# One core, attention and two gated layers: the small inverses' products issued alternately, and an order of issue of its own for every attention row

## The chip, the cores and the metric

One core of a Trainium2 chip. The time is the device time of one execution in microseconds (us). Engines: TensorE (PE, its weight loads PEld), VectorE (DVE), ScalarE (ACT), GpSimd (POOL), SyncE (SP, which issues most DMAs). Each engine works through its own queue in order.

## What is computed

A delta-rule attention over 4 x 8 heads, 768 steps, head size 48, then two feed-forward layers over 3072 tokens of width 384.

```python
for t in range(S):                                   # attention, k normalised
    y[:, :, t] = q[:, :, t] @ state
    v_old = k_n[:, :, t] @ state
    state += beta[:, :, t] * outer(k_n[:, :, t], v[:, :, t] - v_old)
...
xn = x / rms * rms_g                                 # layer 1: 384 -> 1536 -> 384
x = (silu(xn @ w_gate) * (xn @ w_val)) @ w_out
...
h = x @ w_in                                         # layer 2: 384 -> 2048 -> 384
out = (h * tanh(softplus(h))) @ w_out
```

The weights arrive as 64-bit floats and are split on the chip into a high and a low 32-bit part; each large product is three matmuls (high x high, low x high, high x low).

## The kernel before

The 768 steps are cut into 12 rows of 64 steps (r = 0 to 11), two rows making a group (sg = 0 to 5). Inside a row the recurrence becomes the inverse of a 64x64 triangular matrix per head, 32 of them, built from the Gram matrix of the keys (`products`, L578). The inverse of the 32x32 diagonal blocks is built lane by lane on VectorE, and 32x32 products on TensorE put the blocks together:

- For groups 0 and 1 `quick_lane` (L761) goes only to 16x16 blocks on VectorE; `quick_products(r)` (L847) then makes the rest on TensorE in five steps: off x Yd and `Zq` (L861 to L865, with one VectorE addition); YT x Zq (two strips, L867), two copies on ScalarE; Zq x YT (strips 32 and 96, L879) with two copies, and the opening product of `merge32` (L739) with two copies; Zq x YT (strips 0 and 64, L884) with two copies; the closing product of `merge32` (L749) with two copies, which sets ("Y", r).
- For groups 2 to 5 `inlane` (L631) makes 32x32 blocks on VectorE, and `merges` (L890) runs `merge32` for both rows of the group: open, close, open, close, each 32 products and two copies. These steps are called from within `lanes` (L897), one for every two units of the next group's lane.

A product of 32 rows occupies one of four 32-row strips of the array (partitions 0, 32, 64, 96). `merge32` uses two strips at a time, off x Yd all four.

`chain_row(r)` (L914) is a row of attention in named stages: q0, q1 (transposes of q), r (residual), y (state x q), p (masked scores: L600 on TensorE, mask L610 on VectorE), v (`values`, needs ("Y", r)), o0, o1 (outputs), k (state update), s and x (scaling and transposes to the layer's input, done a row later as S, T, X, Y), nA, nB (norms of row r+4's keys), c0, c1, g (its transposes and Gram products). The order of the stages is the string of P: R0, R1, R2, ROW for rows 3 to 9, RL for 10 and 11.

The order of issue is written out by a planner. For rows 0 and 1 `plan` (L44) always issues the stream with the lowest due time; the due times stand in P (`ROW0`, `ROW1`, `QP` for `quick_products`, `L` for the two quick lanes, `CV` for weight conversion, `FF` for part A). From row 2 on `merge` (L62) interleaves streams in proportion to their totals: the row, part A's budget (`DUE`), the conversion of weights, and the lane (`until`, with total `LANE`). Part A is the first third of layer 1 (two of the six slices of 256 hidden columns, gate, value and output weights) for all 12 blocks of 256 tokens; it runs between the attention's products. Weight conversion (`prepare_half`, L152) takes a half at a time: load, absolute value (ScalarE, L168), four operations on VectorE (L172 to L183), the high part cast (ScalarE, L194) and the low part (GpSimd or VectorE, L197). In rows 10 and 11 and the tail it converts the rest of layer 1's weights, which phase B (`phase_b2`, the other four slices) uses from about 460 us on; phase C (layer 2) follows.

Of the kernel before, what the change touches and what calls it, by code (L numbers as in the profile page):

```python
# [20 lines left out]
    XB=2, WE=16, RB=4, TB=4, LANE=18.8, AFTER=6.2, LD=3.0, CVT=9.0, CVB0=0, CVB1=64.0, PSD=1, NU=4, LAG=4, XD=9, PD=12, SQ=5,  # L21
    ROW="r nA q0 q1 S p T nB y X v Y k c0 o0 c1 o1 g".split(),
    R0="r q0 q1 p v k o0 o1 s0 s1 x0 x1 c0 c1 g".split(),
    R1="r nA q0 q1 y p nB v k o0 o1 s0 s1 x0 c0 c1 g".split(),
    R2="r nA Y q0 q1 p nB y v k c0 o0 c1 o1 g".split(),
    RL="r q0 q1 S p T y X Y v o0 k o1".split(),
    DUE=[0, 6, 5, 11],
    CVS=[0, 0, 6.5, 0],
    C=dict(n=0.2, q=0.5, r=1.4, y=1.1, p=1.2, v=1.2, o=0.9, k=1.2, s=0.1, x=0.45, c=0.4, d=0.4, g=1.2, h=1.2),

    ROW0=[24.0, 24.1, 24.4, 46.4, 46.6, 48.6, 49.5, 50.0, 51.0, 51.5, 52.0, 54.0, 62.0, 62.5, 90.0],
    ROW1=[52.5, 54.5, 55.0, 55.5, 56.0, 57.0, 60.0, 60.5, 62.5, 63.5, 64.0, 65.0, 65.5, 66.0, 84.0, 84.5, 90.5],
# [5 lines left out]
    CV=[21.0, 22.0, 23.0, 73.2, 74.8, 76.4, 77.8, 77.9, 78.0] + [79.5 + 0.9 * i for i in range(40)],  # L38
    K1=[7.3, 9.95, 10.0, 10.6], K23=[11.95, 13.2, 15.1, 16.0], K4=[30.0, 47.0, 50.2, 53.0], S=[0, 11.0, 22.0, 23.0, 54.0],
    T=[9.9, 13.0, 25.5, 26.0], G=[12.0, 15.0, 27.5, 28.0], BL=29.0, CVN=12.9,  # L40
# [58 lines left out]
def kernel(  # L99
# [243 lines left out]
    def phase_b1():  # L343
# [234 lines left out]
        def products(r):  # L578
            if r >= NR:
                return  # L580
            sg, rl = divmod(r, 2)
            if rl == 0:
                need(*([("v", r - 5)] if sg > 2 else []))
                A_t[sg] = As[sg % 3]
            need(("T", r, 0), ("T", r, 1))
            gram(("G", r), kT_t[r], kT_t[r], None, A_t[sg][:, rl * 16:rl * 16 + 16, :], swap=True)
            yield 1
# [143 lines left out]
        def merge32(r, X11, Z):  # L731
# [4 lines left out]
            for i in range(16):  # L736
                for e in range(2):
                    o = e * 64
                    nc.tensor.matmul(  # L739
                        ps[o + 32:o + 64, i, :], A[o:o + 32, rl * 16 + i, 32:64], X11[o:o + 32, i, :]  # L740
                    )
            for o in (32, 96):
                nc.scalar.copy(Z[o:o + 32], ps[o:o + 32])
            yield 1.5
            ps = bank(16, 32)
            for i in range(16):
                for e in range(2):
                    o = e * 64
                    nc.tensor.matmul(  # L749
                        ps[o:o + 32, i, :], Z[o + 32:o + 64, i, :], A[o + 32:o + 64, rl * 16 + i, 32:64]  # L750
                    )
# [3 lines left out]
            yield 1.5  # L755

# [4 lines left out]
        def quick_lane(sg):  # L761
# [14 lines left out]
            offs = [t[:, 544:1056].rearrange("p (u c) -> p u c", c=32) for t in (N_, X_)]  # L776
            for rl in range(2):
# [31 lines left out]
            for rl in range(2):  # L809
                r = 2 * sg + rl  # L810
                Nv, Xv = Nw[:, rl], Xw[:, rl]
                for x, y, d in (
# [30 lines left out]
                )  # L843
                halves[r] = [t.rearrange("p (u c) -> p u c", c=32) for t in (Yd, YT)] + [offs[rl]]
                yield 1.75

        def quick_products(r):  # L847
# [5 lines left out]
            def small(lhsT, rhs, groups=(0, 32, 64, 96), ps=None):  # L853
                if ps is None:
                    ps = bank(16, 32)
# [535 lines left out]
```

## Time and profile before

| | us |
|---|---|
| median of 3 runs (lowest, highest) | 1177.6 (1176.66, 1181.1) |
| profiled execution | 1181.6 |
| its span, first to last instruction | 1179.9 |
| TensorE busy in the span | 1112.7 (94%) |
| VectorE, ScalarE, GpSimd busy | 615.0, 387.3, 408.4 |
| mean granted TensorE clock | 0.949 |

A granted clock of 1.00 is 2.4 GHz, of 0.50 is 1.2 GHz; a value between is a mixture over the stretch. Matmuls are pipelined, so an engine that shows busy all the time may still be waiting for the rate of issue. In a line such as `L858 PE MATMUL pp<-A,Zq`, L858 is the line of the kernel, pp the tile written, A and Zq the tiles read; a 32-bit product shows as two records, so a pass of 32 products in the code counts 64. "issue" is a wait for nothing that the profile shows. An interval in brackets at the end of a row is idle time before it and what ended it.

### The profile page before, as it was taken

Reading aid. Unit: us, or ns where it says so; the run is one execution under the profiler, and the core shown is the slowest. Engines: PE = TensorE matmul, PEld = TensorE weight load, DVE = VectorE, ACT = ScalarE, POOL = GpSimd, SP = SyncE. Lnnn points to the kernel's source line nnn. Section 1 sums busy time; section 2 is a strip of 40 time slices with the busy share of each in tenths; the row PEclk is TensorE's granted clock in tenths of the full one; section 3 lists DMA queues with packets and bytes.
Section 4 is the critical chain, followed back from the end, with each engine's and each line's share of the span. In section 5 each row is a group of like instructions: output and inputs, shape, how many; then the busy total and the mean of one; then the engine's idle time right before and its main releaser. Section 6 shows DMA issues by size and latency. Waiting matters only on the chain.

```text
span 1179.9 us, 33143 instructions
## 1 busy us (share of the span) xinstructions
PE 1112.7 (94%) x14712; PEld 1083.1 (92%) x14712; DVE 615.0 (52%) x1039; ACT 387.3 (33%) x822; POOL 408.4 (35%) x364
## 2 busy tenths in 40 slices
PE   5678779999999889999999999999999999999998
PEld 5677678989898889999999999999999999999998
DVE  6656798898987988777676732221111111111111
ACT  4365735676656663222222210111111111111110
POOL 2021035455432442444444432243333333333331
PEclk8656788999999999999999999999999999999999
DMA  9031323333324554443446432611110101111101
GB/s 165 3 70 42 111 56 83 83 90 80 80 83 132 155 203 159 127 142 122 130 139 204 159 122 81 228 54 41 41 41 31 27 25 41 41 41 41 41 1 27
DMA packets 130847, 104.48 MB, mean 89 GB/s; under 512 B 81008, under 2 KB 113264, under 8 KB 130704
## 3 DMA queue, kind: packets, MB, share of 16 engines
q1 hardware_dynamic: 118608, 78.77, 24.0%
q10 hardware_dynamic: 12096, 23.60, 6.1%
q8 instruction: 115, 1.88, 0.7%
q14 instruction: 28, 0.23, 0.1%
HBM read 69.31 MB, written 33.03 MB: 87 GB/s over the span
## 4 chain that ended last, share of the span: by engine, by line
PE 79%; DVE 14%; ACT 2%; SPq 2%; issue 2%; POOL 1%; DMA 0%; DVEq 0%; POOLq 0%; ACTq 0%
PE ph L260 6%; PE ph L259 6%; PE ph L261 6%; PE pd L1322 6%; PE pd L1323 6%; PE pd L1321 6%; PE pg L259 4%; PE pv L259 4%; PE pd L293 4%; PE pg L260 4%; PE pg L261 4%; PE pd L294 4%; PE pd L295 4%; PE pv L261 4%; PE pv L260 4%; DVE pr L658 2%
## 5 line engine op out<-in xcount | busy, mean ns | idle before, releaser
L1309 POOL TENSOR_TENSOR gl<-t,gh 128x512 fp32r<-128x512 f32 x96 | 123.9, 1291 | 266.0 <-DVE gh L1308 266.0
L1308 DVE CAST gh<-t 128x512 fp32r<-128x512 f32 x96 | 43.5, 456 | 328.8 <-ACT t L1303 328.8
L321 POOL TENSOR_TENSOR hl<-sg,hh 128x512 fp32r<-128x512 f32 x72 | 104.5, 1451 | 231.2 <-DVE hh L320 229.8
L1303 ACT ACTIVATE t<-ph 128x512 f32<-128x512 f32 x96 | 57.5, 599 | 346.7 <-PE ph L261 343.1
L260 PE MATMUL ph<-xl,wih 128*128 128x256 f32 x576 | 161.7, 281 | 0.0
L259 PE MATMUL ph<-xh,wih 128*128 128x256 f32 x576 | 161.6, 281 | 0.0
L261 PE MATMUL ph<-xh,wil 128*128 128x256 f32 x576 | 161.5, 280 | 0.0
L1322 PE MATMUL pd<-wql,gh 128*128 128x384 f32 x384 | 129.7, 338 | 0.0
L1323 PE MATMUL pd<-wqh,gl 128*128 128x384 f32 x384 | 129.6, 338 | 0.0
L1321 PE MATMUL pd<-wqh,gh 128*128 128x384 f32 x384 | 129.5, 337 | 0.0
L259 PE MATMUL pv<-xh,wvh 128*128 128x256 f32 x432 | 127.0, 294 | 2.2 <-DVE sg L317 2.2
L259 PE MATMUL pg<-xh,wgh 128*128 128x256 f32 x432 | 127.1, 294 | 0.0
L260 PE MATMUL pg<-xl,wgh 128*128 128x256 f32 x432 | 123.4, 286 | 1.4 <-POOL xl L1071 1.3
L261 PE MATMUL pg<-xh,wgl 128*128 128x256 f32 x432 | 123.0, 285 | 1.5 <-DVE wgl L197 1.5
L261 PE MATMUL pv<-xh,wvl 128*128 128x256 f32 x432 | 123.2, 285 | 1.2 <-DVE wvl L197 1.2
L293 PE MATMUL pd<-hh,woh 128*128 128x256 f32 x420 | 120.5, 287 | 3.0 <-DVE xl L1063 1.5
L260 PE MATMUL pv<-xl,wvh 128*128 128x256 f32 x432 | 123.0, 285 | 0.0
L311 ACT ACTIVATE sg<-pg 128x512 f32<-128x512 f32 x72 | 43.2, 601 | 236.5 <-PE pg L261 215.9
L294 PE MATMUL pd<-hl,woh 128*128 128x256 f32 x420 | 119.0, 283 | 0.0
L295 PE MATMUL pd<-hh,wol 128*128 128x256 f32 x420 | 118.7, 283 | 0.0
L261 PEld LDWEIGHTS ph<-xh,wil 128*128 128x128 f32 x576 | 108.6, 188 | 0.0
L260 PEld LDWEIGHTS ph<-xl,wih 128*128 128x128 f32 x576 | 108.4, 188 | 0.0
(208 smaller groups left out, 2617.7 us busy)
## 6 DMA issues: line engine op xcount, KB each, us to landing
raw<-in_moe_w_out_dram SPq DMA_DIRECT2D x28, 384.0 KB, 3.1
raw<-in_moe_w_in_dram SPq DMA_DIRECT2D x16, 384.0 KB, 4.5
kh<-in_k_dram SPq DMA_DIRECT2D x24, 192.0 KB, 3.9
qp<-in_q_dram SPq DMA_DIRECT2D x24, 192.0 KB, 3.6
v<-in_v_dram SPq DMA_DIRECT2D x48, 96.0 KB, 3.1
raw<-in_moe_w_gate_dram SPq DMA_DIRECT2D x12, 384.0 KB, 4.0
raw<-in_moe_w_val_dram SPq DMA_DIRECT2D x12, 384.0 KB, 3.6
xh_d<-xh SPq DMA_DIRECT2D x12, 384.0 KB, 2.4
```

The source lines that it names most:

```text
L259: nc.tensor.matmul(ps[:, f, :], wh[:, kt, sl], xh[:, kt, :], start=(kt == 0), stop=False)
L260: nc.tensor.matmul(ps[:, f, :], wh[:, kt, sl], xl[:, kt, :], start=False, stop=False)
L261: nc.tensor.matmul(ps[:, f, :], wl[:, kt, sl], xh[:, kt, :], start=False, stop=(kt == KD - 1))
L293: nc.tensor.matmul(ps, wh[:, f, sl], hh[:, f, :], start=(i + f == 0), stop=False)
L294: nc.tensor.matmul(ps, wh[:, f, sl], hl[:, f, :], start=False, stop=False)
L295: nc.tensor.matmul(ps, wl[:, f, sl], hh[:, f, :], start=False, stop=last)
L321: nc.gpsimd.tensor_tensor(out=hl, in0=sg, in1=hh.bitcast(F32), op=ALU.subtract)
L1303: nc.scalar.activation(out=t, in_=ps, func=ACTF.Mish)
L1309: nc.gpsimd.tensor_tensor(out=gl, in0=t, in1=gh.bitcast(F32), op=ALU.subtract)
L1321: nc.tensor.matmul(ps, gh[:, f, sl], wh[:, f, :], start=(m + f == 0), stop=False)
L1322: nc.tensor.matmul(ps, gh[:, f, sl], wl[:, f, :], start=False, stop=False)
L1323: nc.tensor.matmul(ps, gl[:, f, sl], wh[:, f, :], start=False, stop=last and f == 1)
```

## The change

The products: `woven` issues several lists of products alternately, two of each in turn. In `quick_products` YT x Zq (strips 0, 64) and Zq x YT (32, 96) go as one woven pass into one bank with four copies behind; the opening product and Zq x YT (0, 64) as a second one; the closing product stands alone. Five steps become four. In `merges` the closing product of the group's first row is woven with the opening product of its second: four steps become three. The number of products is the same.

```diff
-        def merge32(r, X11, Z):
...
+        def woven(*lists):
+            for i in range(0, max(len(x) for x in lists), 2):
+                for x in lists:
+                    for out_, lhsT, rhs in x[i:i + 2]:
+                        nc.tensor.matmul(out_, lhsT, rhs)
+
+        def closing(r, Z, beside=()):
...
+            ps = bank(16, 32)
+            woven([
+                (ps[o:o + 32, u, :], Z[o + 32:o + 64, u, :], A[o + 32:o + 64, rl * 16 + u, 32:64])
+                for u in range(16) for o in (0, 64)
+            ], beside)
             for o in (0, 64):
                 nc.scalar.copy(A[o:o + 32, us, 32:64], ps[o:o + 32])
             done.add(("Y", r))
...
+            woven(small(ps, YTv, Zq, (0, 64)), small(ps, Zq, YTv, (32, 96)))
             for o in (0, 64):
+                copy(X11[o:o + 32], ps[o:o + 32])
             for o in (32, 96):
                 copy(A[o:o + 32, us, 32:64], ps[o:o + 32])
+            yield 2.4
+            ps = bank(16, 32)
+            woven(small(ps, A[:, us, 32:64], X11, (0, 64), 32), small(ps, Zq, YTv, (0, 64)))
+            for o in (32, 96):
+                copy(X11[o:o + 32], ps[o:o + 32])
             for o in (0, 64):
                 copy(A[o:o + 32, us, 0:32], ps[o:o + 32])
             yield 2.0
+            closing(r, X11)
...
         def merges(sg):
+            A, X11 = A_t[sg], X11_t.pop(sg)
+            Zs = [X11[:, rl * 16:rl * 16 + 16] for rl in range(2)]
...
+            ps = bank(16, 32)
+            woven(opening(0, ps))
+            keep(0, ps)
+            yield 1.5
+            ps = bank(16, 32)
+            closing(2 * sg, Zs[0], opening(1, ps))
+            keep(1, ps)
+            yield 1.5
+            closing(2 * sg + 1, Zs[1])
+            yield 1.5
```

The order: P gets a string for every row (R0 to R11), new due times for `plan`, a budget for part A for every row (`DUE`), a rate of the lane for every row (`LR` in place of `LANE`), and lists that say which engine does the copies of part A's sums (`PDR`), the low parts of x (`XDR`) and the parts of weight conversion (`FAV`, `BAV`, `BLV`). The lane of group 2 starts within `plan` (its first step), and part A's tail is merged at another rate (`PF`). Some `need` lines are added; they are conditions that are asserted while the program is built, and they issue nothing.

```diff
-    XB=2, WE=16, ..., XD=9, PD=12, SQ=5,
-    ROW="r nA q0 q1 S p T nB y X v Y k c0 o0 c1 o1 g".split(),
-    RL="r q0 q1 S p T y X Y v o0 k o1".split(),
-    DUE=[0, 6, 5, 11],
...
+    LN0=0.036,
+    LNT=(103.416, 0.567),
+    FAV=[0, 0, 1, 0, 0, 0],
+    XDR=[0, 0, 0, 0, 0, 0, 0, 0, 0, 0, 1, 1],
+    PDR=[0, 0, 0, 0, 0, 0, 0, 1, 0, 0, 1, 1],
+    BLV=[0, 0, 0, 0, 1, 0, 0, 1, 0, 1, 0, 0],
+    BAV=[0, 1, 1, 1, 1, 1, 1, 1, 0, 1, 0, 1],
+    PF=[4.593, 58.969, -0.713, 9.632, 6.207],
...
+    R0="q0 q1 p r v k o0 o1 s0 s1 x0 c0 c1 x1 g".split(),
+    R1="r nA q0 q1 y p nB v o1 k o0 s0 s1 x0 c0 c1 g".split(),
+    R2="r nA q0 Y nB q1 v p y c0 c1 k o0 o1 g".split(),
+    R3="r nA q0 q1 S p T X nB y v Y k c0 o0 c1 g o1".split(),
...
+    R11="q0 r S q1 p T y X Y v o0 o1 k".split(),
+    DUE=[0.917, 5.474, 4.22, 10.835, 10.74, 11, 11, 10.41, 11, 10.528, 10.133, 10.44],
+    LR=[-10.273, 15.158, 18.8, 7.185, 18.693, 16.183, 18.8, 18.8, 21.092, 19.69, 19.49, 24.92],
...
-    QP=[
-        [39.5, 41.0, 42.2, 43.4, 44.6], [45.3, 46.3, 47.3, 48.3, 49.3],
-        [66.0, 68.0, 70.0, 71.5, 73.0], [73.2, 75.0, 76.5, 78.0, 79.5],
-    ],
-    L=[(20.0, 1.08), (46.5, 1.15)], FF=(80.5, 3.2),
+    QP=[[37.093, 34.452, 40.408, 45.783], [45.3, 46.477, 51.275, 43.34], [64.123, 71.417, 67.286, 67.117], [74.991,
+        76.5, 78, 79.5]],
+    L=[(18.111, 1.09), (44.665, 1.15)],
+    FF=(80.625, 11.746),
...
-                    streams.append((until(lane, laned, upto), P["LANE"]))
+                    streams.append((until(lane, laned, upto), P["LR"][r]))
...
-        run(budget(part_a, 3))
+        run(budget(part_a, P["PF"][0]))
...
-        merge((part_a, 19.0), (seq(budget(cv, P["CVT"]), delay(1)), P["CVT"] + 1))
+        merge((part_a, P["PF"][1]), (seq(budget(cv, P["CVT"]), delay(P["PF"][2])), P["CVT"] + 1))
```

In `plan` a stream's next due time is the entry of its list with the number of steps that it has issued so far, so an entry lower than its predecessor means that the step follows at once.

## Rows read from the trace of the kernel before

**Rows 1.** Stages, in time from:to and length; then PE, PEld, DVE, ACT, POOL busy, clock, DMA

```profile
40.00:125.00 85.00, 66.15 (x2336) 61.13 (x2337) 50.11 (x85) 45.15 (x99) 14.22 (x18) 0.56 0.21 50
125.00:205.00 80.00, 64.15 (x1292) 59.06 (x1292) 74.02 (x115) 43.20 (x95) 28.07 (x23) 0.85 0.32 81
205.00:360.00 155.00, 153.04 (x3760) 141.63 (x3759) 138.30 (x185) 103.00 (x243) 71.03 (x55) 1.00 0.32 81
360.00:460.00 100.00, 89.55 (x1451) 83.69 (x1450) 85.69 (x152) 59.15 (x139) 37.62 (x38) 0.97 0.50 162
460.00:1180.00 720.00, 715.42 (x5460) 715.09 (x5458) 237.83 (x423) 117.68 (x212) 251.25 (x212) 1.00 0.26 83
```

**Rows 2.** Chain of waits: start us, us, what

```profile
46.83 3.29 PE pp L858 x120
...
183.70 1.89 DVE pr L658
```

**Rows 3.** VectorE's waits, 40 to 130 us: total us, times, longest

```profile
DVE Zq L863 <- PE pp L858: 16.4, 2, 8.8
DVE v L945 <- PE pp L940: 6.5, 1, 6.5
DVE compq L627 <- ACT compq L626: 3.2, 1, 3.2
DVE sx L1037 <- PE pp L1032: 3.0, 2, 2.3
```

**Rows 4.** Timeline of TensorE: start us, us, line, operation

```profile
41.25 1.93 PE L858 MATMUL pp<-A,N__178 32*32 32x32 f32 x128 [4.22 <-DVE A L833]
...
46.83 1.76 PE L858 MATMUL pp<-Zq,A 32*32 32x32 f32 x58 [3.65 <-DVE Zq L863]
...
98.02 1.29 PE L858 MATMUL pp<-A,N__178 32*32 32x32 f32 x128
...
123.48 0.58 PE L259 MATMUL pg<-xh,wgh 128*128 128x256 f32 x1
```

**Rows 5.** Timeline of ScalarE, 48 to 63 us

```profile
48.79 1.18 ACT L875 COPY X11q<-pp 32x512 f32<-32x512 f32 x2 [10.66 <-PE pp L858]
...
62.68 1.15 ACT L626 ACTIVATE compq<-A,h 128x1024 f32<-128x1024 f32 x1
```

**Rows 6.** Timeline of VectorE, end of group 1's lane

```profile
104.19 1.04 DVE L841 STREAM_TRANSPOSE A<-e 128x512 f32<-128x512 f32 x1
```

**Rows 7.** Groups of instructions by shape: busy us, mean ns

```profile
L197 POOL TENSOR_TENSOR wvl<-t,wvh 128x384 fp32r<-128x384 f32 x8 | 8.9, 1115 | 13.2 <-ACT wvh L194 13.2
...
L1257 DVE CAST yh<-par 128x256 fp32r<-128x256 f32 x36 | 11.2, 312 | 1.9
...
L1063 DVE SCALAR_TENSOR_TENSOR xl<-pp,gT,xh 128x128 fp32r<-128x128 f32 x18 | 5.1, 343 | 2.4 <-ACT xh L1060 2.4
...
L197 DVE TENSOR_TENSOR wvl<-t,wvh 128x384 fp32r<-128x384 f32 x4 | 2.2, 555 | 3.0 <-ACT wvh L194 3.0
```

**Rows 8.** Timeline of VectorE, row 3

```profile
185.50 1.29 DVE L610 TENSOR_TENSOR PT<-pp,mpos 128x512 f32<-128x512 f32 x2
...
194.56 1.01 DVE L1037 TENSOR_TENSOR sx<-sx,pp 128x384 f32<-128x384 f32 x2
```

**Rows 9.** Timeline of ScalarE, end of group 2's lane

```profile
204.08 1.05 ACT L727 COPY A<-yc 32x1024 f32<-32x1024 f32 x1
```

**Rows 10.** Timeline of TensorE, first merge product

```profile
206.52 1.20 PE L739 MATMUL pp<-X,A 32*32 32x32 f32 x64
207.65 0.39 PE L293 MATMUL pd<-hh,woh 128*128 128x256 f32 x1
```

**Rows 11.** One line on VectorE, 385 to 460 us: ns min/median/max

```profile
L175 DVE TENSOR_SCALAR t<-t x20: 359/361/1345, 385.2 to 457.3; 128x384 int32<-128x384 int32 x20
```

**Rows 12.** Timeline of ScalarE, row 11

```profile
407.44 0.55 ACT L168 ACTIVATE t<-raw 128x384 f32<-128x384 f32 x1 [3.54 <-POOL wvl L197]
```

**Rows 13.** TensorE's waits, 40 to 130 us

```profile
PE pp L858 <- issue: 4.1, 3, 1.5
```

More of the change, by code (lines that the diff above doesn't have):

```diff
@@ L776, in quick_lane @@
             offs = [t[:, 544:1056].rearrange("p (u c) -> p u c", c=32) for t in (N_, X_)]
+            if sg:
+                need(("off", 0), ("off", 1))
             for rl in range(2):
@@ L851, in quick_products, with small @@
             Ydv, YTv, off = halves.pop(r)
-            def small(lhsT, rhs, groups=(0, 32, 64, 96), ps=None):
-                if ps is None:
-                    ps = bank(16, 32)
-                for u in range(16):
-                    for o in groups:
-                        nc.tensor.matmul(ps[o:o + 32, u, :], lhsT[o:o + 32, u, :], rhs[o:o + 32, u, :])
-                return ps
-            ps = small(off, Ydv)
+            def small(ps, lhsT, rhs, groups, shift=0):
+                return [
+                    (ps[o + shift:o + shift + 32, u, :], lhsT[o:o + 32, u, :], rhs[o:o + 32, u, :])
+                    for u in range(16) for o in groups
+                ]
+            copy = nc.scalar.copy
+            ps = bank(16, 32)
+            woven(small(ps, off, Ydv, (0, 32, 64, 96)))
             Zq = flat(hp.tile([128, 2, T], F32R, tag="hl", name="Zq")).rearrange("p (u c) -> p u c", c=32)
@@ L865, in quick_products @@
             )
+            done.add(("off", r))
             yield 2.8
-            ps = small(YTv, Zq, (0, 64))
             if rl == 0:
@@ L887, in quick_products, with opening, keep @@
             yield 2.0
-            yield from m32
+            closing(r, X11)
+            done.add(("hq", r))
+            yield 2.0
         def merges(sg):
-            X11 = X11_t.pop(sg)
-            for rl in range(2):
-                us = slice(rl * 16, rl * 16 + 16)
-                Z = kp.tile([128, 16, 32], F32, tag="Z", name="Z")
-                yield from merge32(2 * sg + rl, X11[:, us], Z)
+            A, X11 = A_t[sg], X11_t.pop(sg)
+            Zs = [X11[:, rl * 16:rl * 16 + 16] for rl in range(2)]
+            def opening(rl, ps):
+                return [
+                    (ps[o + 32:o + 64, u, :], A[o:o + 32, rl * 16 + u, 32:64], X11[o:o + 32, rl * 16 + u, :])
+                    for u in range(16) for o in (0, 64)
+                ]
+            def keep(rl, ps):
+                for o in (32, 96):
+                    nc.scalar.copy(Zs[rl][o:o + 32], ps[o:o + 32])
+            ps = bank(16, 32)
+            woven(opening(0, ps))
+            keep(0, ps)
+            yield 1.5
+            ps = bank(16, 32)
+            closing(2 * sg, Zs[0], opening(1, ps))
[3 more added lines that the diff above has]
+            yield 1.5
         def lanes(ending):
+            need(("off", 2), ("off", 3), ("ql", 3))
             nc.gpsimd.memset(X_, 0.0)
@@ L994, in outputs @@
                 need(("v", r), ("p", r), ("y", r) if r else ("p", r))
+                if r == 0 and bp:
+                    need(("o", r, 0))
                 if r == 0 and bp == 0:
@@ L1116, in finish_a @@
         def finish_a(r):
+            need(("hq", 2), ("hq", 3))
             par = tp.tile([128, KD, T], F32, tag="par", name="par", bufs=1)
             def finish(o, ps):
-                (nc.vector.tensor_copy if r >= P["PD"] else nc.scalar.copy)(par[:, o, :], ps)
+                (nc.vector.tensor_copy if P["PDR"][r] else nc.scalar.copy)(par[:, o, :], ps)
                 if o == KD - 1:
@@ L1169, in phase_b1 @@
         run(warm(24), norms([0], sq[2:]), scale_first(0))
+        lane, laned, left = lanes(iter(())), [0.0], []
         plan(
@@ L1183, in phase_b1 @@
             (budget(part_a, P["DUE"][1]), P["FF"]),
+            (until(lane, laned, P["LN0"]), P["LNT"]),
         )
-        lane, laned, left = lanes(iter(())), [0.0], []
         for sg in range(1, NSEG):
```

106 lines of the change are left out of this document (58 added, 48 removed), and 3 rows, old and new, of the table CV.

## The prediction

> **What bounds the kernel now.** I read the stage table first [rows 1]. From 460 us on TensorE is busy without a gap (715.4 of 720 us) at the upper clock, and nothing in the change touches that code, so this part stays at 720 us. What can move is the first 460 us, and it has four regimes. From 40 to 125 us no engine is full: TensorE is busy for 66 of 85 us at a granted clock of 0.56, VectorE for 50. From 125 to 205 us VectorE is full (74 of 80). From 205 to 360 us TensorE is full (153 of 155) with VectorE close behind (138). From 360 to 460 us TensorE has 10 us of idle time and VectorE 14.
>
> The chain of waits [rows 2] says the same in order of time: the inverses' products on TensorE at 46.8 us, VectorE's lane operations up to 185.6 us, then TensorE. The list of waits adds who is late in the first regime: VectorE stands still for 16.4 us in two waits for the first product (Zq), 6.5 for row 1's residual, 3.2 for ScalarE's `compq`, 3.0 for the state updates [rows 3].
>
> **The change part by part.** The sum is made against the profiled execution: 1181.6 us, of which the span is 1179.9. The median of the runs is 1177.6, 4.0 us less; I take the same difference off both.
>
> *Early weaving.* A pass is 32 products in the code and 64 records in the trace. The pass of 46.83 us uses two of the four 32-row strips: 58 records in 1.76 us, 30 ns each. The pass of 41.25 us goes through all four strips: 128 records in 1.93 us, 15 ns each [rows 4], in the same stretch of low granted clock. So two woven passes cost what one costs, and each weaving saves about 1.7 us. There are two weavings for each of rows 0 to 3: 8 x 1.7 = 13.6 us of TensorE time. But the chain is product, copy, product: the next product needs ScalarE's pair of copies (1.18 us [rows 5], with the hand-overs about 1.4). Today another pass runs meanwhile; after weaving nothing is left to cover it, twice a row: 8 x 1.4 = 11.2 us. Alone, the weaving gives 13.6 - 11.2 = 2.4 us.
>
> Two pages of the Trainium skill speak against even that. "TensorE: Matmul & The Clock Gate" (section "Wait — 56ns, not 53.3ns?") says that start-to-start never drops below about 25 ns, however narrow the product; then a woven pair of 128 records would take 3.2 us, as two passes do now, the lost cover would stand alone, and by an estimate from that page the sum would come out some 12 us higher, near 1180. The 15 ns of the four-strip pass [rows 4] contradict it. "TensorEngine Tiling (Array Packing)" (section "Restrictions and Gotchas") says that different row tiles cannot access the same PSUM bank at once; both woven lists write one bank, and by that rule they would take turns, with the same result. The four-strip pass writes one bank too and runs at twice the rate [rows 4], so the trace does not bear it out here.
>
> *New due times, 40 to 125 us.* Sorting the old and new due times by hand gives the order of issue. Today the first product of row 1 stands behind all five steps of row 0, and `ql1.diag` (the start of lane group 1) behind row 1's second step on ScalarE. After the change `ql1.diag` comes before row 1's first product, and row 0's closing after it. The pass that needs Zq starts near 45 us (46.8 today [rows 4]), since Zq waits for one lane step fewer; with two passes of 1.7, a covering gap of 1.4 and four copies (2.4) ScalarE is free for `ql1.diag` at about 52 us, in place of 62.7 [rows 5]. The lane of group 1 ends at 105.2 us today [rows 6]. Of the 55 us after 50 us VectorE idles 8.8 + 6.5 + 3.2 + 3.0 = 21.5 [rows 3] and works 33. New idle time by my walk through the order: 3.4 (for `ql1.diag`), 1.7 (state update of row 0), 5 (residual of row 1, now behind two transposes), 4 (mask of row 1), 2 (state update of row 1), that is 16, and some 2 us of the later pieces slip, so the lane ends near 101. Row 2's products then no longer wait until all else is done: its chain (5.1 of passes, 2.8 of copies) runs from 98.4 to 106, row 3's from 106 to 116 (1.0 + 1.2 for Zq, then 7.9). Part A's first matmul stands at 123.5 [rows 4], so it comes 7 us earlier. In the VectorE-bound stretch that follows, the weight pair moved from ScalarE to VectorE costs 2 halves x (0.36 to 0.56 + 0.31 to 0.56), about 1.6 us [rows 7, 11]: lead 5.4.
>
> *Rows' orders, 125 to 205 us.* In row 3 the lane's share is issued late (rate 7.2 in place of 18.8). The mask of p comes forward by the lane pieces put behind it, about 2.9 us, but between mask and state update (185.5 to 194.6 us) fewer lane pieces are left to fill VectorE, so about 4.5 us of idle time appear there, and the lane's end (ScalarE's last copy at 204.1, first merge product at 206.5) [rows 8 to 10] has only 1.4 us of slack. TensorE's lead is therefore capped near the merge of row 4. Bounds: -10 (lead, mask gain and the 1.6 of the moved pair hidden) and +3 (4.5 less the slack, no lead). I take -5 for everything before 205 us, nearest to the 5.4 worked out.
>
> *Merges, 205 to 385 us.* Per group four passes of 64 records become three; each takes 1.20 us, the next matmul beginning 1.13 after the start [rows 10]. Four groups: 4 x 1.13 = 4.5 us, three of them where TensorE is full [rows 1]. Bounds -4.5 and 0 (if VectorE, 138 of 155 us, takes over). I take -3.9.
>
> *Rows 9 to 11.* The converted weights of phase B and the copies change engine. VectorE gains: one pair's abs and cast, 1.7; four low parts at 0.56, 2.2; row 10's three `par` copies at 0.31, 0.9. It loses six subtractions of row 9 at 0.34, 2.1 [rows 7]. Net +2.7 of VectorE time. GpSimd loses four low parts at 1.1. Where GpSimd runs beside it, the same VectorE instruction takes up to 1.35 us in place of 0.36 [rows 11], so fewer GpSimd operations give about 2 us back. ScalarE loses a 3.5 us wait for GpSimd's low part that held up q's copies [rows 12]. I take -2, bounds -6 and +4.
>
> *Tail.* The last conversions of the merge (`cw17` on, some 5 halves) now come after part A's last matmuls, ahead of phase B's first gating on VectorE. A half is four VectorE operations between 0.36 and 0.56 us, about 1.8, and 0.5 of cast or low part [rows 7, 11]: 11.5 us of backlog. Cover: phase B's matmuls into four PSUM buffers, 4 x 18 x 0.13 (715 us over 5460 matmuls [rows 1]), 9.4 us. Today these halves lie between part A's units. I take +1, bounds -1 and +5.
>
> Sum: -5 - 3.9 - 2 + 1 = -9.9. The profiled execution would be 1171.7; on the median, 1177.6 - 9.9 = **1167.7**.
>
> The other edits (the order of norms and transposes before 41 us, the `need` lines, rates that round to the same number of steps: part A still gives 6, 5 and then 11 units a row) I set at nothing: the lane of group 0 on VectorE covers them and keeps its length; uncovered, the moved transpose of q ahead of row 1's Gram product would cost about 0.6 us.
>
> **The rivals.** *Clock.* In 40 to 125 us the granted clock is 0.56 on average, so nearly all at 1.2 of the two levels 1.2 and 2.4 GHz [rows 1]. If the closer-packed work is granted the upper level, each of the remaining passes shrinks by a third or more (the four-strip pass took 1.29 us at 98 us in place of 1.93 [rows 4]): 16 passes of the products and some 8 of rows 0 and 1, x 0.6 = 14 us, of which half on the chain, -7, with -5 from the 24 us at the lower level between 125 and 205 (mean 0.85): 1167.7 - 12 = 1156. For it: bursts at the upper level exist. Against it: the gaps for copies remain.
>
> *Weaving does not do what it says.* TensorE already waits 4.1 us in three pieces for "issue" in the same stretch [rows 13]: if its instructions arrive no faster than 30 ns apart, woven passes take as long as two. Then the merges give 0, the early lead falls by 2 weavings x 1.7 for rows 2 and 3 each (6.8) to +1.8, and the rest stays: +1.8 - 2 + 1 = +0.8, so about 1178. Against it stands the four-strip pass at 15 ns [rows 4]. The two rules of the Trainium skill named above ("TensorE: Matmul & The Clock Gate", "TensorEngine Tiling (Array Packing)") would lead to this case.
>
> *Slower: the backlog at the hand-over to phase B.* VectorE arrives at 460 us with its 2.7 us of added work and the 11.5 us of late conversions; TensorE runs out of PSUM buffers 9.4 us after part A's end. It decides once VectorE and GpSimd block one another there: 10 instructions lengthened by 1 us each [rows 11] make the backlog 21.5 us, a stall of 12, with +4 from rows 9 to 11 in place of -2. With -5 and -3.9 still earned: 1177.6 + 7 = 1185.
>
> **How the numbers follow.** Forecast 0.53, clock 0.18, no weaving gain 0.20, slower 0.09. About 0.5% (5.9 us) is what a measurement of this kernel can tell from no change, so faster means under 1171.7. Of the forecast's cases 0.85 are under it: 0.45; clock 0.18; of the third 0.15: 0.03. Faster 0.66. Slower is the last rival less a fourth of it, 0.07; the rest, 0.27, is no change. The range for 8 in 10: low end from the clock rival less part of the open bounds in rows 9 to 11, 1153; high end just above the third case, 1180.
>
> **What would show it.** Right: part A's first matmul near 116.5 us in place of 123.5; VectorE's waits for Zq under 10 us; 128 woven records in under 2 us; three merge passes a group and row pairs in 205 to 360 us shorter by 1.1; the first merge product some 5 us earlier. Wrong: new "issue" waits inside woven passes; TensorE idle before the first merge; waits of phase B's first blocks on VectorE; the lane of group 1 ending after 105. If part A starts 7 us earlier but row 4 does not, the lane's end took it; if the lead at row 4 is above 10 us, I undersized the VectorE-bound stretch.

## The result: 10.6 us less, all of it earned before 190 us

| | before | after |
|---|---|---|
| median (lowest, highest), four runs each | 1179.35 (1176.66, 1181.38) | 1168.77 (1168.46, 1169.33) |
| profiled execution, its span | 1181.6, 1179.9 | 1168.46, 1166.7 |
| mean granted clock | 0.949 | 0.954 |

The ratio is 0.9912, with an interval of 0.9887 to 0.9937. The forecast was 1167.7, made as 9.9 us less than a median of 1177.6; with the fourth run that median is 1179.35.

The stages of the kernel after, in the columns of [rows 1]:

```profile
40.00:125.00 85.00, 61.47 (x2492) 54.74 (x2493) 58.32 (x105) 50.69 (x109) 14.97 (x20) 0.62 0.25 64
125.00:205.00 80.00, 66.97 (x1542) 61.06 (x1543) 74.63 (x118) 43.93 (x96) 30.26 (x24) 0.85 0.30 71
205.00:360.00 155.00, 149.84 (x3554) 137.61 (x3549) 138.52 (x179) 99.28 (x239) 70.80 (x57) 1.00 0.35 94
360.00:460.00 100.00, 90.08 (x1380) 85.21 (x1372) 84.49 (x161) 49.21 (x120) 35.26 (x35) 1.00 0.51 160
460.00:1180.00 720.00, 702.17 (x5346) 701.82 (x5346) 232.24 (x414) 114.94 (x208) 251.77 (x213) 1.00 0.25 80
```

The reader is to see two things. VectorE does 8.2 us more work between 40 and 125 us than in [rows 1] (58.3 against 50.1). From 40 us to the end of group 2's lane its work is nearly the same in both kernels, 122.5 and 121.1 us, but it has 28.9 us of idle time beside it where it had 39.4 (columns as in [rows 1]; before, then after):

```profile
40.00:201.86 161.86, 127.17 (x3545) 117.12 (x3545) 122.50 (x197) 85.23 (x191) 42.29 (x41) 0.69 0.27 66
```

```profile
40.00:189.96 149.96, 117.61 (x3635) 105.89 (x3636) 121.05 (x201) 84.16 (x187) 40.79 (x41) 0.72 0.29 72
```

And TensorE has 5.2 us of idle time between 205 and 360 us where it had 2.0. (In the last row the span ends at 1166.7; TensorE is as full there as before, all but 4.5 us.)

VectorE's waits between 40 and 130 us, in the columns of [rows 3]:

```profile
DVE sx L1100 <- PE pp L1095: 4.6, 2, 3.8
DVE Zq L903 <- PE pp L778: 4.4, 1, 4.4
DVE compq L669 <- ACT compq L668: 3.8, 1, 3.8
DVE wgl L237 <- ACT wgh L234: 3.4, 1, 3.4
DVE t L212 <- ACT t L208: 3.3, 1, 3.3
DVE v L1006 <- PE pp L1001: 3.2, 1, 3.2
DVE PT L652 <- PE pp L642: 1.6, 1, 1.6
```

The two waits for Zq of 16.4 us have become one of 4.4. The seven rows sum to 24.3 us (a last one of 0.5 lies behind them); the list of before sums to 33.9, with 4.8 us in three waits for ScalarE's conversions beside [rows 3]. Three rows of ScalarE's timeline answer [rows 5] and [rows 9]: `compq`, the start of lane group 1, at 51.4 in place of 62.7 us, and the first of the three copies that end group 2's lane. [rows 9] shows the last of the three; the first one of before stands in the second fence.

```profile
45.77 1.18 ACT L916 COPY X11q<-pp 32x512 f32<-32x512 f32 x2 [7.64 <-PE pp L778]
...
51.37 1.15 ACT L668 ACTIVATE compq<-A,h 128x1024 f32<-128x1024 f32 x1
...
189.96 1.04 ACT L767 COPY A<-yc 32x1024 f32<-32x1024 f32 x1 [2.29 <-DVE yc L765]
```

```profile
201.86 1.04 ACT L725 COPY A<-yc 32x1024 f32<-32x1024 f32 x1
```

TensorE's timeline answers [rows 4]: the first woven pass, two products of each list in turn, the wait for the copy behind it, and part A's first matmul (123.48 in [rows 4]).

```profile
43.79 0.26 PE L778 MATMUL pp<-Zq,A 32*32 32x32 f32 x2 [2.48 <-DVE Zq L903]
43.80 0.26 PE L778 MATMUL pp<-A,Zq 32*32 32x32 f32 x2
...
45.47 0.24 PE L778 MATMUL pp<-A,Zq 32*32 32x32 f32 x2
46.40 0.31 PE L778 MATMUL pp<-X11q,A 32*32 32x32 f32 x2 [0.68 <-ACT X11q L916]
...
115.90 0.58 PE L299 MATMUL pg<-xh,wgh 128*128 128x256 f32 x1
```

From 43.79 to 45.71 the pass of 128 records takes 1.92 us, 15 ns each, as the four-strip pass in [rows 4]; issued one list behind the other, in the kernel e1_not_woven below, the same 128 take 3.45 us. TensorE's waits between 40 and 130 us show the price, the answer to [rows 13]:

```profile
PE pp L778 <- issue: 7.4, 7, 1.5
PE pp L778 <- DVE Zq L903: 3.3, 2, 2.5
PE pp L778 <- ACT X11q L923: 3.3, 6, 1.0
PE pp L778 <- ACT X11q L916: 2.9, 6, 0.7
```

Three of the seven waits for "issue" lie inside woven passes, the later part of which begins so:

```profile
57.98 0.26 PE L778 MATMUL pp<-Zq,A 32*32 32x32 f32 x2 [1.44 <-issue]
...
107.35 0.26 PE L778 MATMUL pp<-Zq,A 32*32 32x32 f32 x2 [0.76 <-issue]
...
111.90 0.27 PE L778 MATMUL pp<-X11q,A 32*32 32x32 f32 x2 [1.11 <-issue]
```

### Where the lead is made: four stretches in every trace

The end of one stretch is the start of the next: TensorE's first matmul of part A; ScalarE's first copy at the end of group 2's lane; the same copy of group 5; the first activation of phase C (`Mish`). The last one, with its following 95, reads in the kernel after and in a second trace of the kernel before (group rows: ns min/median/max, first and last start):

```profile
L1369 ACT ACTIVATE t<-ph x96: 597/597/600, 749.8 to 1151.8; 128x512 f32<-128x512 f32 x96
```

```profile
L1303 ACT ACTIVATE t<-ph x96: 597/598/600, 760.2 to 1162.2; 128x512 f32<-128x512 f32 x96
```

Lengths in us, worked out from such rows of each profiled execution:

| kernel | 40 us to first A | to group 2's end | to group 5's end | to phase C | ratio to before (interval) |
|---|---|---|---|---|---|
| before, two traces | 83.5; 80.9 | 78.4; 78.4 | 167.8; 167.9 | 393.3; 393.0 | 1 |
| after | 75.9 | 74.1 | 168.0 | 391.9 | 0.9912 (0.9887, 0.9937) |
| e1_not_woven | 81.1 | 74.3 | 167.6 | 392.2 | 0.9977 (0.9962, 0.9992) |
| e2_weave_only | 83.2 | 77.6 | 169.0 | 393.7 | 1.0057 (1.0041, 1.0072) |
| e3_tail_rate_back | 74.7 | 74.2 | 166.3 | 393.2 | 0.9942 (0.9925, 0.9958) |
| e4_plan_only | 75.5 | 74.0 | 169.4 | 391.0 | 0.9917 (0.9903, 0.9932) |
| e12_late_lane | 80.6 | 74.1 | 168.8 | 392.2 | 0.9938 (0.9914, 0.9962) |
| e13_merges_apart | 78.3 | 74.4 | 169.7 | 393.8 | 0.9922 (0.9897, 0.9946) |
| e10_plan_weights | 77.9 | 75.3 | 170.3 | 391.0 | 0.9923 (0.9904, 0.9943) |
| e11_group2_short | 76.6 | 71.9 | 168.1 | 393.3 | 0.9900 (0.9880, 0.9920) |

The table says how far one trace can be trusted. Seven kernels have the code of the kernel after up to part A (after, e3, e5, e6, e7, e11, e13); their first stretch lies between 74.7 and 78.3, with 76.1 in the middle. Five of them have the same code behind group 5's end (after, e5, e7, e11, e13); their fourth stretch lies between 391.9 and 393.8. The second stretch is the same in all with the new plan, within 0.4 us, where nothing in it was changed.

So the lead is 82.2 - 76.1 = 6.1 us in the first stretch (the middle of before's two traces), 4.3 in the second, nothing in the third: 10.4, against 10.6 between the medians. The 1.3 of this trace in the fourth is within the scatter there.

How the lead divides between the first two stretches depends on where their border falls. Before, all but one of VectorE's waits for ScalarE's conversions end behind part A's first matmul; after, the one of 3.3 us (`DVE t L212` above) ends at 115.80, 0.1 us ahead of it, and 0.9 us of waits are left in the second stretch. Its waits in the second stretch before (123.5 to 201.9 us):

```profile
DVE wvl L197 <- ACT wvh L194: 3.0, 2, 2.2
DVE t L172 <- ACT t L168: 1.2, 1, 1.2
```

So 3.3 of the 4.3 us are VectorE's waits, 4.2 against 0.9; its work there is 73.0 and 71.4 us.

### The profile page after: what moved, and what is told of

Its sections match the earlier page's. It is cut to its first block, busy times and chain, and to the rows that moved or that the text cites. A ratio compares the mean times of both kernels' runs of the same rounds, so it can differ in the third digit from the quotient of the medians.

```text
span 1166.7 us, 33125 instructions
## 1 busy us (share of the span) xinstructions
PE 1096.5 (94%) x14712; PEld 1064.1 (91%) x14712; DVE 618.5 (53%) x1056; ACT 377.3 (32%) x803; POOL 409.3 (35%) x368
## 4 chain that ended last, share of the span: by engine, by line
PE 66%; DVE 7%; issue 1%; DMA 0%; ACT 0%; POOL 0%; DVEq 0%; POOLq 0%
PE ph L300 6%; PE ph L299 6%; PE ph L301 6%; PE pd L1388 6%; PE pd L1389 6%; PE pd L1387 6%; PE pd L333 3%; PE pd L334 3%; PE pv L299 3%; PE pd L335 3%; PE pv L301 3%; PE pv L300 3%; PE pg L299 3%; PE pg L301 3%; PE pg L300 3%; DVE t L220 1%
```

## The experiments

Ratios go by the runs of the kernel before on the same chip, whose median was 1177.4 for e1 to e4, 1179.8 for e5 to e7, and 1180.2 for e10 to e13.

### Weaving and order, one without the other

*The new order, not woven.* The lists are issued one behind the other.

```diff
-            for i in range(0, max(len(x) for x in lists), 2):
-                for x in lists:
-                    for out_, lhsT, rhs in x[i:i + 2]:
-                        nc.tensor.matmul(out_, lhsT, rhs)
+            for x in lists:
+                for out_, lhsT, rhs in x:
+                    nc.tensor.matmul(out_, lhsT, rhs)
```

> The changed kernel with every step and due time kept, but the lists of a woven pass issued one after the other. Theory A (the gain comes from where the steps stand; a woven pass only trades TensorE time for uncovered copies): about 2 us over the changed kernel, 1170 to 1173, the first matmul of part A at most 3 us later than 115.9. Theory B (the gain is the weaving: 8 x 1.7 us early and 4 x 1.13 in the merges): 10 us or more lost, 1179 to 1183.

Measured: 1174.14 us. *Weaving with the old order:* the due times, strings, rates and engines of before, the woven passes and four steps of after.

```diff
-    L=[(18.111, 1.09), (44.665, 1.15)],
+    L=[(20.0, 1.08), (46.5, 1.15)],
-    QP=[[37.093, 34.452, 40.408, 45.783], [45.3, 46.477, 51.275, 43.34], ...
+    QP=[[39.5, 41.0, 42.2, 43.4], [45.3, 46.3, 47.3, 48.3], ...
...
```

> The woven products with all orders, rates, due times and engines of the kernel before (four of the five due times of each quick product). Theory A: close to the kernel before, 0 to 4 us faster, part A's first matmul at 120 to 124 us. Theory B: nearly the whole gain, 1168 to 1171, part A's first matmul near 116.

Measured: 1183.93 us. Neither theory stands alone: 1174.14 lies between their ranges, and 1183.93 above both. The order without weaving gives 0.2% (3 us), weaving without the order loses 0.6%, both together give 0.9%. TensorE's row for 40 to 125 us in the weaving-only kernel and its waits between 40 and 130 us (L771 is the woven product there) show why weaving alone earns nothing:

```profile
40.00:125.00 85.00, 58.48 (x2337) 51.63 (x2338) 49.05 (x84) 45.03 (x98) 14.54 (x18) 0.56 0.21 50
```

```profile
PE pp L771 <- issue: 6.7, 8, 1.2
PE pp L771 <- ACT X11q L916: 4.7, 8, 1.4
PE pp L771 <- ACT X11q L909: 3.0, 6, 0.7
```

Against [rows 1] TensorE is busy for 7.7 us less at the same clock. Its waits for the copies rise from 0.4 us (one wait for X11q in the trace of before) to 7.7, those for "issue" from 5.2 (4.1 of [rows 13] and one of 1.1) to 6.7: 8.8 us back. In the new order the same weaving is worth about 5 us, all of it before part A (81.1 against 74.7 to 78.3): VectorE waits less for what TensorE and ScalarE bring early. These two rows of VectorE's waits in the not woven kernel stand against 3.8 and 4.4 after:

```profile
DVE compq L669 <- ACT compq L668: 6.8, 1, 6.8
DVE Zq L902 <- PE pp L777: 6.5, 2, 6.0
```

### The early start of one lane

TensorE's order is the same as after, instruction for instruction; only the second quick lane's due time goes back, and with it `compq` behind six more ScalarE copies.

```diff
-    L=[(18.111, 1.09), (44.665, 1.15)],
+    L=[(18.111, 1.09), (46.5, 1.15)],
```

> The kernel after, with one due time changed: the second quick lane begins at 46.5 in the planner's list, as before, in place of 44.665. TensorE's order is the same instruction for instruction. On ScalarE the lane's first operation (compq) stands behind six more copies of row 1's products and two of row 0's state update, so the lane of group 1 starts some 4 to 7 us later (52.5 us in the kernel after). Theory P (the gain before 125 us is VectorE's idle time, taken out by starting this lane early): the lane's last step comes 3 to 6 us later than 95.5 us, part A's first matmul 3 to 6 us later than 115.9, the lead over the kernel before shrinks by as much in all later stages, and the time is 1171 to 1174. Rival W (the gain comes from the woven products, wherever the lane starts): less than 1 us, 1167 to 1170.

Measured: 1173.88 us. VectorE's use of `compq` (L669) moves from 52.5 to 63.0 us, where it was in the kernel before (63.9), and its wait grows from 3.8 to 9.7 (VectorE's waits, 40 to 130 us):

```profile
DVE compq L669 <- ACT compq L668: 9.7, 1, 9.7
```

Group 1's lane ends 6.0 us later, part A begins 4.7 later, and 5.9 are left at phase C; by the ratios it is 0.26%, 3 us. Theory P holds: one number of the plan carries 3 to 6 us, without a change in any product.

### The planned part alone

Rows 2 to 11 get back their old strings, budgets, rates and engines, and part A's tail its old rate; the woven products and the plan up to row 1 stay.

```diff
-    R3="r nA q0 q1 S p T X nB y v Y k c0 o0 c1 g o1".split(),
+    R3="r nA q0 q1 S p T nB y X v Y k c0 o0 c1 o1 g".split(),
...
-    DUE=[0.917, 5.474, 4.22, 10.835, ...
+    DUE=[0, 6, 5, 11, ...
-    PF=[4.593, 58.969, -0.713, 9.632, 6.207],
+    PF=[3, 19.0, 1, 13.0, 7.0],
```

> The changed kernel up to row 1 (new due times, woven products) with the orders, rates and engines of before from row 2 on and in the tail. If the lead is made in the planned part, before row 2, and kept: r of row 2 near 129 us and 1170 to 1173. If the new orders of rows 2 and 3 make it (lead 8.7 us at row 2, 11.6 at row 5): lead at row 5 of 6 or less and 1174 to 1178.

Measured: 1167.44 us, below both ranges, and the ratio of the kernel after within 0.0005. The title's second half, an order for every row, earns nothing that can be measured beyond rows 0 and 1. *The tail's rate alone:*

```diff
-    PF=[4.593, 58.969, -0.713, 9.632, 6.207],
+    PF=[4.593, 19.0, 1, 9.632, 6.207],
```

> The changed kernel with the rate of the tail as before (part A's last 17 units spread over the conversions again). If the waits of TensorE at phase B's start (2.4 us for sg on ScalarE, 1.6 us for sg on VectorE) come from the conversions put behind part A, they go and 3 to 4 us are gained, 1165 to 1166. If these waits are paid back anyway (part A's own last steps slowed by the conversions again), no change within 1.5 us.

Measured: 1169.75 us. The ratio is 0.3% higher, the profiled execution 1.4 us shorter than that of after: no gain that can be told apart. The two waits of 2.4 and 1.6 us are gone, and others of the same sum have come: TensorE's waits from 360 to 470 us are 9.7 us, against 9.9 after.

### Weights back on ScalarE

To the planned part alone, the pair of weights that the change moved goes back: two absolute values and two casts.

```diff
-    FAV=[0, 0, 1, 0, 0, 0],
+    FAV=[0, 0, 0, 0, 0, 0],
```

> The kernel with the new plan of rows 0 and 1 and the woven products, all else as before (1167.4 us), and also with the first six halves of the weights as before: one pair of absolute value and cast goes back from VectorE to ScalarE (four operations, 1.4 to 1.8 us of VectorE work between 125 and 190 us). Theory V2: what VectorE saves there comes off the whole: 1165.5 to 1166.5. Rival: the casts stand behind part A's first activation in ScalarE's queue, the low parts wait for them, and the time is 1168 to 1171.

Measured: 1172.11 us, no gain. The second stretch is 1.3 us longer (75.3 against 74.0, one trace of each) though VectorE has four operations fewer and 1.3 us less work there (70.9 against 72.2): it stands behind ScalarE's cast, a wait that the kernel with the pair on VectorE does not have in this stretch (VectorE's waits from 117.9 to 193.2 us):

```profile
DVE wgl L230 <- ACT wgh L227: 2.6, 1, 2.6
```

### Is VectorE the bound, and where?

*From part A to group 2's end.* Group 2's lane leaves out 2.6 us of VectorE work.

```diff
+            if sg != 2:
                 nc.vector.tensor_tensor(
                     out=Nv, in0=Nv, in1=bl[:, sg, :].unsqueeze(1)..., op=ALU.mult
                 )
...
+            if sg != 2:
                 nc.vector.tensor_tensor(
                     out=Nv, in0=Xv, in1=bl[:, sg, :].unsqueeze(2)..., op=ALU.mult
                 )
```

> The kernel after, but the lane of group 2 alone leaves out VectorE's two multiplications by beta (2.6 us of VectorE work, between 125 and 190 us; this part of the computation is left out). In groups 3 to 5 the same omission moved nothing. Theory V2 (from 125 to 190 us VectorE's work alone sets the pace, and what is gained there stays until the end): the end of group 2's lane (ScalarE's copy at 190.0) comes 2.6 us earlier, each later lane's end too, and the time is 1165 to 1167. Rival T2 (the merge of the next row, or part A on TensorE, is as late as the lane): the lane's end moves by 2.6 us and the ends of groups 3 to 5 by less than 1, the time stays at 1168 to 1169.

Measured: 1169.16 us, ratio 0.9900. The second stretch is 2.2 us shorter (71.9), as theory V2 says: there VectorE sets the pace. Of the 2.2, 2.1 are left at group 5's end, counted from part A's start, and 0.7 at phase C. V2's time, 1165 to 1167, did not come; the ratio can't tell 2.6 us from none.

*From 205 to 360 us.* The same omission in groups 3 to 5, and in another kernel a third of the up projections' matmuls left out in blocks 2 to 8:

```diff
-            nc.vector.tensor_tensor(
-                out=Nv, in0=Nv, in1=bl[:, sg, :].unsqueeze(1)..., op=ALU.mult
-            )
+            if sg < 3:
+                nc.vector.tensor_tensor(
...
```

> The kernel after, but the lanes of groups 3 to 5 leave out VectorE's two multiplications by beta (rows by columns of a 32 by 32 block; about 1.22 and 1.35 us each, so 2.6 us of VectorE work in each group; this part of the computation is left out). From 190 us to about 360 us the kernel after repeats a group's lane every 57 us, as before. Theory V (VectorE's work sets that period): the copies that end the lanes of groups 3, 4 and 5 (247, 304 and 358 us in the kernel after) come 2.5, 5 and 7.5 us earlier, the period goes to about 54.5 us and the time to 1161 to 1164. Theory T (TensorE's work sets it): the lane's own results come some 2 us earlier in their row, the period stays 57 us, and the time stays within 2 us of 1168.

```diff
-            nc.tensor.matmul(ps[:, f, :], wl[:, kt, sl], xh[:, kt, :], start=False, stop=(kt == KD - 1))
+            if low:
+                nc.tensor.matmul(ps[:, f, :], wl[:, kt, sl], xh[:, kt, :], start=False, stop=(kt == KD - 1))
...
+                up(pg, W["g", m], 0, xh, xl, low=len(pairs) > FA or not 2 <= n < 9)
```

> The kernel after, but part A's blocks 2 to 8 leave out the product with the low half of the weights in the up projections (24 of 72 matmuls of a block, about 2.9 us of TensorE work in each row, 5.7 us in each group; this part of the computation is left out). VectorE's work is unchanged. Theory V (VectorE's work sets the 57 us period of a group): TensorE idles more, the ends of the lanes of groups 3 to 5 move by less than 2 us each, the time stays within 3 us of 1168. Theory T: the period falls to 51 or 52 us, the end of group 5's lane comes some 17 us earlier, the time goes to 1150 to 1155. Both bind by turns: a period of 54 to 55 us.

One execution each: 1169.44 and 1166.94 us. The row of 205 to 360 us and VectorE's longest wait in it with the short lanes, then the row with the short up projections:

```profile
205.00:360.00 155.00, 149.98 (x3580) 137.98 (x3572) 132.47 (x174) 100.42 (x241) 69.41 (x57) 1.00 0.35 92
```

```profile
DVE v L1009 <- PE pp L1004: 7.9, 6, 1.9
```

```profile
205.00:360.00 155.00, 142.27 (x3470) 128.75 (x3466) 143.32 (x188) 101.31 (x244) 71.65 (x58) 0.96 0.35 95
```

With 6 us less VectorE work (132.5 against 138.5) the period of a group stays at 56.8, 57.5 and 52.5 us (57.1, 57.3 and 53.6 after): VectorE waits longer for TensorE instead, 7.9 us in place of 5.2 for the residual. So theory V is out. With the short up projections TensorE is busy for 14.8 us less in the third stretch (143.8 against 158.6), and the stretch shrinks by 6.0 (162.0), with periods of 55.0, 55.7 and 51.3 us; VectorE's share rises to 143 of 155, the granted clock falls to 0.96, and of the 6.0 only 1.5 are left at phase C. Theory T's price, 17 us and a time of 1150 to 1155, did not come: the third case, both by turns, is nearest. TensorE binds this stretch at first, with VectorE a few us behind. Two things may eat the rest, and no run separates them: the granted clock between 350 and 370 us, 0.77 there against 1.00 after, and VectorE, which is full from 370 to 410 us with the short up projections (38.8 of 40 us) as in the kernel after. One row of the kernel after:

```profile
370.00:390.00 20.00, 19.17 (x406) 17.71 (x401) 19.41 (x33) 15.71 (x42) 11.83 (x14) 1.00 0.62 188
```

*A cast moved off VectorE.* A version meant to be faster: part A's cast of 0.43 us goes to ScalarE, busy for 99 of 155 us, in blocks 0 to 8.

```diff
-                nc.vector.tensor_copy(hh, sg)
+                (nc.scalar.copy if len(pairs) == FA and n < 9 else nc.vector.tensor_copy)(hh, sg)
```

> The kernel after, but the cast of part A's high half (0.43 us, two of them in each row) runs on ScalarE in blocks 0 to 8: 0.86 us of VectorE work less in each row, 1.7 us in each group. Theory V: the period of a group falls from 57 to about 55.3 us, the hand-over to the next phase comes about 6 us earlier, the time goes to 1162 to 1166. Theory T: nothing, 1166 to 1170. A rival against the edit: ScalarE's queue holds the cast back, the low half behind it and the down projection of the block are late by 1 to 2 us in a row, and the time goes to 1170 to 1178.

Measured: 1187.99 us, ratio 1.0072 (1.0047, 1.0097), some 19 us behind the kernel after. The rival against the edit holds, and far above its price. ScalarE's and VectorE's longest wait between 205 and 360 us:

```profile
ACT hh L360 <- DVE sg L357: 30.9, 9, 7.1
```

```profile
DVE v L1006 <- PE pp L1001: 13.6, 5, 6.7
```

The cast waits at the head of ScalarE's queue for VectorE's product (up to 7.1 us), and the copies behind it, which attention needs, wait with it: VectorE's waits for the residual go from 5.2 to 13.6 us. Two groups take 61.5 and 67.2 us.

### The merges apart

Only the merges' two lists are issued one behind the other; steps, bank and copies stay.

```diff
-            ], beside)
+            ])
+            if beside:
+                woven(beside)
```

> The kernel after, but in the merges of groups 2 to 5 the closing products of the first row and the opening products of the second are issued one list behind the other; the bank, the copies and the three steps stay, and so do the woven products of rows 0 to 3. This gives back about 1.1 us of TensorE time in each of four groups. If the merges' weaving is worth what it saves on TensorE, the time is 1172 to 1173 (4.5 us more). If other work covers it, since TensorE has 5 us of idle time between 205 and 360 us in the kernel after: TensorE's busy time there rises by 2 to 3.4 us, its idle time falls by as much, the ends of the lanes stay within 0.5 us, and the time stays at 1168 to 1169.5. The not woven kernel, whose lead was constant from part A's first matmul on, speaks for the second.

Measured: 1170.99 us, ratio 0.9922. The third stretch is 1.8 us longer than after (169.7). That is no more than the scatter between traces of the same code there (166.3 in e3, whose change lies behind it, to 168.8 in e12), and the not woven kernel has 167.6. The merges' weaving is worth something between 0 and 2 us, not 4.5.

### The kernel before, once more

> The kernel before, once more, for a second trace of it. Its executions lie between 1176 and 1182 us and the one profiled at first was 1181.6. If this one is near 1177, the two traces beside each other say in which stage the 4 us between executions lie; a comparison with the kernel after has to leave that stage's difference out. Expected: the stages up to 460 us agree within 1 us, and the difference lies behind it, at a slightly different granted clock.

One execution: 1178.83 us; span 1177.1 against 1179.9. It was expected that the stages up to 460 us agree within 1 us; they do not: of the 2.8 us, 2.6 lie before part A. The rows of 60 to 80 us, first trace and second:

```profile
60.00:80.00 20.00, 18.19 (x540) 16.81 (x537) 7.89 (x12) 15.09 (x34) 4.51 (x9) 0.50 0.23 43
```

```profile
60.00:80.00 20.00, 17.60 (x528) 15.98 (x524) 9.03 (x14) 16.25 (x40) 4.95 (x9) 0.63 0.22 43
```

At a granted clock of 0.63 in place of 0.50 the same products end earlier. The profile on which the prediction rests was one of the longer executions, so the lead in its first stretch (7.6 us) is 1.3 us too large by the middle of the two.

## Why the prediction was right, and which of its steps were not

The time came out within 1.1 us of the forecast by luck, because two errors cancelled: the part before 205 us gave 5.4 us more than forecast, and the merges 3.9 less.

- **Early weaving, right in both halves, too high in size.** It was worked out as 13.6 us of passes saved and 11.2 of uncovered copies, 2.4 net. With the old order the runs show 7.7 saved and 8.8 lost in waits, nothing net. Some passes ran at the upper clock already (1.29 us for the four-strip pass of 98.02 in [rows 4]), so there was less to save. A woven pass takes 1.92 us ("128 woven records in under 2 us"). The two rules that spoke against it, the floor of about 25 ns between starts (the Trainium skill, "TensorE: Matmul & The Clock Gate", section "Wait — 56ns, not 53.3ns?") and row tiles that cannot use one bank at once ("TensorEngine Tiling (Array Packing)", section "Restrictions and Gotchas"), do not set the pace in this trace: 128 records go into one bank at 15 ns each. The prediction took the floor as one between records. Counted by products, two records each, the 15 ns are 30, which a floor of 25 would allow; the four-strip pass of 98.02 in [rows 4] took 10 ns a record and 20 a product, which it would not by either count.
- **Due times, right at both ends, not on the way.** Part A's first matmul was forecast at 116.5 and came at 115.9, `ql1.diag` at 52 and came at 51.4 on ScalarE; the waits for Zq are under 10 us. That the lane's early start carries it is shown by e12. But lane group 1 ended at 96.5 us, not near 101, and row 3's products took from about 101 to 116 us in place of 106 to 116, with 3.1 us of waits for "issue" inside the passes from 103 us on; that the two make up for each other is luck.
- **125 to 205 us, wrong in sign.** This is the step that failed: the lead of 7 was to shrink, by 1.6 for the pair of weights moved to VectorE and by the merge at row 4. It grew by 4.3 us. VectorE waits 3.3 us less there, as shown with the table. Part of that is the pair on VectorE, which saves 1.3 us (e10), since VectorE no longer waits for ScalarE's cast. And VectorE's conversions run faster. Three groups of this stretch (busy us, mean ns), 123.5 to 202 us before and 115.9 to 190 us after:

```profile
L172 DVE TENSOR_SCALAR t<-t 128x384 f32<-128x384 f32 x9 | 4.3, 477 | 1.2 <-ACT t L168 1.2
L197 DVE TENSOR_TENSOR wol<-t,woh 128x384 fp32r<-128x384 f32 x4 | 4.0, 1026 | 0.0
L175 DVE TENSOR_SCALAR t<-t 128x384 int32<-128x384 int32 x9 | 4.0, 442 | 0.3
```

```profile
L215 DVE TENSOR_SCALAR t<-t 128x384 int32<-128x384 int32 x9 | 3.2, 360 | 0.3
L237 DVE TENSOR_TENSOR wol<-t,woh 128x384 fp32r<-128x384 f32 x4 | 3.2, 806 | 0.0
L212 DVE TENSOR_SCALAR t<-t 128x384 f32<-128x384 f32 x9 | 3.2, 351 | 3.3 <-ACT t L208 3.3
```

  The same 22 instructions take 2.7 us less. That they met GpSimd's work less often is the likely cause, as in [rows 11]: of the 18 of L172 and L175 before, the 14 with no GpSimd instruction beside them take 0.36 us in the mean, the four with one for over half their time 0.82; after, two have one, and take 0.37. So not every meeting costs, and no run isolates it. With both stretches the term "everything before 205 us" was 10.4, not 5; it lies just past the bound of 10 for the gain. This is the case for which the prediction says "I undersized the VectorE-bound stretch". The first merge product was to come some 5 us earlier; it came 16.0 earlier (206.52 in [rows 10]):

```profile
190.47 1.20 PE L778 MATMUL pp<-X,A 32*32 32x32 f32 x64
```

- **Merges, mis-sized.** The forecast took 3.9 of the bounds 4.5 and 0. They gave nothing that can be told from none. The sign set for them, row pairs shorter by 1.1, did not come (57.1, 57.3 and 53.6 us against 56.9, 56.3 and 54.5). TensorE's busy time fell (163.5 to 158.6 us in the third stretch), and idle time took its place (4.3 to 9.4). The end at 0 was meant for VectorE taking over; e5 shows that VectorE's work is not the bound either. The longest new wait is for ScalarE's copy `par`, which stands in its queue behind the copies that end group 2's lane:

```profile
194.69 0.40 PE L333 MATMUL pd<-hh,woh 128*128 128x256 f32 x1 [3.02 <-ACT par L1184]
```

  No run isolates it, and the planned part alone, which does not have it, is no shorter in this stretch (169.4).
- **Rows 9 to 11 and tail, right by accident.** Together -1 forecast, -1.3 measured in the fourth stretch, which is within the scatter there; and the planned part alone, with the old engines and rate, has -2.1. So the new engines and the new rate earn nothing that can be seen. The tail's backlog shows as two waits at the hand-over, but TensorE's waits from 360 to 470 us sum to 9.9 us as before (10.1). The two:

```profile
PE pg L299 <- ACT sg L351: 2.4, 1, 2.4
...
PE pv L299 <- DVE sg L357: 1.6, 1, 1.6
```

- **The rivals.** The clock of the first stage rose to 0.62, against 0.56 and 0.60 in the two traces of before, so no 12 us came from it. New "issue" waits did appear (7.4 us against 5.2), and three of them, 3.3 us, inside woven passes, which was set down as a sign of being wrong; but the passes without a wait run at 15 ns a record, so the rival's mechanism, no two passes in the time of one, is out. The kernel before has 1.5 us of such a wait inside a pass too. The slower case did not come: no wait at the hand-over is above 2.4 us.

What stays open: which due time brings VectorE's waits for the conversions ahead of part A, where TensorE's idle time in the third stretch comes from, and why weaving alone measures 0.6% slower (6.6 us between medians). Its trace equals the first trace of before, one of the longer executions, within 1 us in every stretch but the third (1.2); against the second trace it is 3.4 us longer, 2.4 of them before part A.

No run beat the kernel after by more than the runs tell apart; the planned part alone is as fast, with far fewer tuned numbers.

## What to carry to other kernels

Sum the idle time of the engine that will be full in the next stage: here the plan gained what it took out of that sum (39.4 to 28.9 us of idle time, 11.9 us of lead in the same trace), and the lead lasted to the end. Packing work on another engine was worth its saving only where that idle engine waited for it; the same woven passes gave 5 us in one order and none in the other. And work moved to an engine with free time can cost more than it frees if it waits at the head of that engine's queue: 18 casts of 0.43 us, moved, made the kernel 19 us longer.

## What the runs showed of the hardware

- Executions of the same code differ by up to 3.6 us in part A's start (114.7 to 118.3). About half of that is there at the end of group 0's lane (its last VectorE transpose begins at 39.3 in the one and 41.2 in the other); the rest comes in a stretch at a mixture of the two clock levels. Two traces of the kernel before had 0.50 and 0.63 in the same 20 us, and their 2.6 us at part A's start were 2.8 at the end. A lead of a few us should be read from stretches at one level, or from several traces.
- When a third of the up projections' matmuls was left out, the granted clock of 205 to 360 us fell from 1.00 to 0.96. Between 330 and 350 us TensorE was busy for 16.6 of 20 us (19.8 in the kernel after), and between 350 and 370 us the granted clock was 0.77. How much of the gain this took back was not measured.
- One-input VectorE instructions of 128x384 took 0.36 us in the mean with no GpSimd instruction beside them and 0.82 with one for over half their time (kernel before, 14 and 4 instructions between 123.5 and 202 us; in the kernel after two such took 0.37).
